# Last feed-forward of a retention and mixture-of-experts kernel: the list scheduler's group time, hand-over times and selection rule

## The chip, the cores and the metric

The kernel runs on one core of a Trainium2 chip. The metric is the device time of one execution in microseconds, as the median of several runs. All times below are microseconds unless marked ns. PE is the matrix engine (TensorE), PEld its weight loads, ACT is ScalarE, DVE is VectorE, POOL is GpSimd and SP is the engine whose queue issues most transfers.

## The reference

The program computes three layers in sequence. The change concerns the third alone, whose width is 512, whose hidden width is 2048, and which has 4608 tokens.

```python
def reference(**kwargs):
    attn_out = _attn_ref(**attn_kwargs)                  # retention, 8 batches x 8 heads x 576 x 64
    x = attn_out.transpose(0, 2, 1, 3).reshape(B * S, H * D)
    x = _moe_ref(x=x, **moe_kwargs)                      # 8 experts, one chosen per token
    return _moe2_ref(x=x, **moe2_kwargs)

def _moe2_ref(x, w_in, w_out):                           # 4608 x 512, 512 x 2048, 2048 x 512
    h = np.maximum(x @ w_in, 0.0)
    return (h * h @ w_out).astype(np.float32)
```

## The kernel before, in words

`phase0` does the retention, `phase12` the experts, `phase3` the last feed-forward. The change lies in `Plan`, the scheduler that `phase3` uses, and in one constant of `phase3`.

**How the work is cut.** `phase3` cuts the tokens into nine tiles of 512 and the hidden width into eight blocks of 256. It goes over the tiles in three passes: pass 0 takes three blocks, pass 1 two and pass 2 three, so that the weights of one pass stay on chip. The second pass goes over the tiles backwards, so the tile at each turn of passes is not loaded again. In pass 0 the tile's input is read, and seven combinations of its four quarters are formed (`xprep`), each split into a high and a low part, by an ACT copy and a DVE subtraction; they are also written to memory (`xc`), from which passes 1 and 2 read them again. Partial outputs go to memory between the passes (`pd`).

**Products.** Each block of a tile is a 2 x 2 block product done with seven products in place of eight, named 1, 2, 6, 5, 7, 4, 3. `one(n, q, x)` makes product x of the first matrix for block q of tile number n, and `two(n, x)` product x of the second matrix. Each is a *group* of six matmuls of 256 columns: two halves, each as high times high, high times low and low times high (lines 1211, 1212 and 1213 of `six`). So a tile has 42 groups in passes 0 and 2, and 28 in pass 1; in all 1008 groups.

**What follows a product.** First products write PSUM banks X (two buffers), Y (two) and Z (one); products 1, 6, 7 and 4 of one block all go through the same X buffer, one after the other. From there ACT copies (L1186) and DVE additions (L1189) form the tile z; it is squared after a relu (`sq`, on DVE as one operation at L1197, or on ACT as two at L1194 and L1195, as the planner chooses), combined (L1189), and split into a high and a low part h (`hsplit`: ACT at L1320, DVE at L1321). z and h have three buffers. Second products read h and write three further banks, X, Y and Z, from which ACT copies or DVE additions bring them into the output tiles `oe` and `yr`. In pass 2 POOL writes finished rows out with indirect transfers (`scatter`).

**The planner.** Nothing of this is issued at once. Each call adds an operation to `Plan.ops`: the engines that can do it with a duration on each, the operations that it must follow (through the names of what it reads and writes), and for transfers a landing time. Durations are formulas: for DVE 0.15 + 0.00106 per column, for ACT 0.21 + 0.00083 per column, for a transfer its size at 320 KB per us plus 2.0 to land, for a group of six matmuls the constant `MMS`. Transfers count as an engine of their own; in the kernel they stand in the queue of SP.

`emit` works in two steps. First it gives each operation a due time. A group of matmuls is due at the sum of the group times in program order ahead of it; another operation is due `SLACK` after that point, and in both cases earlier if what depends on it is due earlier: the due time of the follower, less the operation's duration, landing time and the hand-over to another engine. Then it simulates the engines. An operation among the first 400 that are left is a candidate once all that it must follow has been placed; it can begin when these have ended, with a hand-over added if they ran on another engine, and its engine is free. (`OVER` is the share of an ACT or DVE operation that overlaps the next one.) One candidate is placed at a time, and this selection is part of what the change touches. At the end all operations are issued in the order of their planned starts. On the chip each engine works through its own queue in that order and waits at each operation for what it depends on; the planned times themselves are not used.

Of the kernel before, what the change touches and what calls it, by code (L numbers as in the profile page):

```python
# [92 lines left out]
def kernel(ctx, tc, qT, kT, kN, vN, modT, w_gate, mbias, w1, w2, w_in, w_out,  # L93
# [18 lines left out]
    class Banks:  # L112
        def __init__(self, **tags):
            self.tags = {t: [b, 0] for t, b in tags.items()}
# [974 lines left out]
    AT1 = {1: 0, 2: 1, 6: 3, 5: 5, 7: 6, 4: 9, 3: 11}  # L1089

    class Plan:
        HAND = 0.25
        SLACK = 6.0
        OVER = {"ACT": 0.14, "DVE": 0.11}

        def __init__(self):
            self.ops, self.wrote, self.read = [], {}, {}

        def add(self, engs, fn, r=(), w=(), land=0.0):
            deps = set()  # L1100
            for k in r:
                deps.update(self.wrote.get(k, ()))
            for k in w:
                deps.update(self.wrote.get(k, ()))
                deps.update(self.read.get(k, ()))
            i = len(self.ops)
            self.ops.append((engs, fn, deps, land))
            for k in r:
                self.read.setdefault(k, []).append(i)
            for k in w:  # L1110
                self.wrote[k] = [i]
                self.read[k] = []

        def emit(self, ahead=400, near=0.15):
            n = len(self.ops)
            lat = lambda i: min(t for _, t in self.ops[i][0])
            at, due = 0.0, [0.0] * n
            for i, (engs, _, _, _) in enumerate(self.ops):
                due[i] = at + (0.0 if engs[0][0].name == "PE" else self.SLACK)
                at += engs[0][1] if engs[0][0].name == "PE" else 0.0  # L1120
            for i in range(n - 1, -1, -1):
                engs, _, deps, _ = self.ops[i]
                for d in deps:
                    same = len(engs) == 1 and self.ops[d][0] and self.ops[d][0][0][0] is engs[0][0]
                    due[d] = min(due[d], due[i] - lat(d) - self.ops[d][3] - (0.0 if same else self.HAND))
            free, end, on, starts = {}, {}, {}, []
            todo = list(range(n))
            ready = {}
            while todo:
                cand = []  # L1130
                for i in todo[:ahead]:
                    engs, fn, deps, land = self.ops[i]
                    if i not in ready:
                        if any(d not in end for d in deps):
                            continue
                        ready[i] = [max([end[d] + (0 if on[d] == e.name else self.HAND) for d in deps],
                                        default=0.0) for e, _ in engs]
                    _, s0, e, t = min(((max(r_, free.get(e.name, 0.0)) + t, max(r_, free.get(e.name, 0.0)), e, t)
                                       for (e, t), r_ in zip(engs, ready[i])), key=lambda z: z[:2])
                    cand.append((s0, due[i], i, e, t))  # L1140
                first_ = min(c[0] for c in cand)
                lead = min((c for c in cand if c[0] == first_), key=lambda c: c[1:3])
                s0, _, i, e, t = min((c for c in cand if c[0] <= first_ + near and c[3] is lead[3]),
                                     key=lambda c: c[1:3])
                free[e.name] = s0 + t * (1.0 - self.OVER.get(e.name, 0.0))
                end[i] = s0 + t + self.ops[i][3]
                on[i] = e.name
                starts.append((s0, len(starts), i, e))
                todo.remove(i)
            for s0, _, i, e in sorted(starts, key=lambda z: z[:2]):  # L1150
                self.ops[i][1](e.h)
            self.starts = starts
# [5 lines left out]
    def phase3():  # L1158
        with ExitStack() as c2:
# [3 lines left out]
            for j in (1, 2):  # L1163
# [14 lines left out]
            PE_, ACT_, DVE_, POOL_, DMA_ = (Eng(n_, h_) for n_, h_ in  # L1178
                                            (("PE", pe), ("ACT", act), ("DVE", dve), ("POOL", pool), ("DMA", sp)))
# [28 lines left out]
            def six(ps, pairs, first):  # L1208
                def go(e):
                    for n, ((lh, ll), (rh, rl)) in enumerate(pairs):  # L1210
                        e.matmul(ps[n], lh, rh, start=first and n == 0, stop=False, skip_group_check=True)  # L1211
                        e.matmul(ps[n], lh, rl, start=False, stop=False, skip_group_check=True)  # L1212
                        e.matmul(ps[n], ll, rh, start=False, stop=True, skip_group_check=True)  # L1213
                return go

            MMS = [(PE_, 0.72)]

            def loadw(p, m, j0=0):
                for j, fp in list(enumerate(PASSES[p]))[j0:]:
# [50 lines left out]
            def one(n, q, x):  # L1270
                p, t = T3[n]
                if x == 1:
# [8 lines left out]
                w, m, mx = WT[0][q], MW[x], MX[x]  # L1281
                plan.add(MMS, six([ps, ps], [((w[0][:, m, P * k:P * k + P], w[1][:, m, P * k:P * k + P]),
                                              (XT[mx][:, 0, k, :], XT[mx][:, 1, k, :])) for k in range(2)],
# [48 lines left out]
            def two(n, x):  # L1332
# [4 lines left out]
                for q in range(len(PASSES[p])):  # L1337
                    u = HS_[n, q]
                    h, m, w, mo = HT[u % 3], MH[x], WT[1][q], MO[x]
                    plan.add(MMS, six([ps[:, 0, :], ps[:, 1, :]],  # L1340
                                      [((h[:, 0, m, P * b:P * b + P], h[:, 1, m, P * b:P * b + P]),
# [66 lines left out]
    with tc.manual_schedule():  # L1408
        phase0()
        phase12()  # L1410
        cm.close()
        phase3()
# [37 lines left out]
```

## Time and profile before

| | us |
|---|---|
| median of 3 runs | 1332.95 (1332.58 to 1333.44) |
| the profiled execution | 1330.45 |
| its span, first to last instruction | 1328.7 |
| first matmul of the last feed-forward, from the span's start | 609.7 |
| mean granted TensorE clock | 0.995 |

The span is the time from the first to the last instruction of the profiled execution; the execution's own time is 1.75 longer, and the median of the runs is 2.5 above that. Lines such as L1213 are those of the kernel's listing. A name such as `bank<-x,w` says what an instruction writes and what it reads; in the last feed-forward `x,w` marks first products and `w,h` second products. Matmuls are pipelined, so their durations overlap, and the distance from start to start says how fast they run.

### The profile page before, as it was taken

The numbers are of one execution on the slowest core, as the hardware profiler recorded it, in microseconds if no ns is written. First come the engines' busy times: TensorE is split into PE (matmuls) and PEld (weight loads), VectorE is DVE, ScalarE is ACT, GpSimd is POOL, SyncE is SP. The second block draws the span as 40 slices with busy tenths as digits, with TensorE's granted clock in tenths as the row PEclk, the third lists the DMA queues.
The fourth block names the chain that finished last, engine by engine and source line by source line (L and its number), as shares of the span: only waits on it lengthen the run. The fifth ranks groups of instructions, "written<-read, shape, count | busy, mean of one in ns | idle before, by whom it ended". The sixth has DMA issues, their size and how long they took to land.

```text
span 1328.7 us, 26978 instructions
## 1 busy us (share of the span) xinstructions
PE 1284.4 (97%) x10639; PEld 1196.3 (90%) x10639; DVE 1023.2 (77%) x2095; ACT 623.1 (47%) x1283; POOL 125.3 (9%) x170
## 2 busy tenths in 40 slices
PE   7999989999999999899999999999999999999996
PEld 6888877888888888899999999999999999999996
DVE  3877859878887887665888888867888777777665
ACT  2344444545445444454655556534344344443343
POOL 3222112101100110000000000000000011111121
PEclk9999999999999999899999999999999999999999
DMA  9998257787777877779555554678799866555451
GB/s 330 390 346 300 88 183 245 264 296 272 279 280 264 285 258 270 273 268 351 206 205 221 219 197 175 245 263 309 289 348 345 298 225 211 206 196 175 175 192 47
DMA packets 152499, 331.89 MB, mean 250 GB/s; under 512 B 15440, under 2 KB 67440, under 8 KB 152368
## 3 DMA queue, kind: packets, MB, share of 16 engines
q1 hardware_dynamic: 144752, 309.82, 65.5%
q0 software_dynamic: 5840, 19.14, 4.0%
q8 instruction: 85, 1.39, 0.4%
q10 hardware_dynamic: 1776, 1.17, 0.3%
q14 instruction: 46, 0.38, 0.1%
HBM read 222.33 MB, written 107.78 MB: 248 GB/s over the span
## 4 chain that ended last, share of the span: by engine, by line
PE 40%; DVE 12%; DMA 1%; issue 1%; ACT 0%; POOL 0%; POOLq 0%; DVEq 0%
PE bank L1213 13%; PE bank L1211 13%; PE bank L1212 13%; DVE z L1189 5%; DVE h L1321 3%; DVE z L1197 2%; DMA x<-xc 1%; DVE x L1189 1%; DVE yr L1189 1%; PE bank L839 0%; PE bank L840 0%; PE bank L841 0%; ACT h L1320 0%; DVE oe L1189 0%; POOL out L1328 0%
## 5 line engine op out<-in xcount | busy, mean ns | idle before, releaser
L1211 PE MATMUL bank<-x,w 128*128 128x256 f32 x1008 | 279.6, 277 | 7.5 <-ACT z L1186 5.4
L1212 PE MATMUL bank<-x,w 128*128 128x256 f32 x1008 | 279.4, 277 | 4.4 <-DVE x L1189 4.4
L1211 PE MATMUL bank<-w,h 128*128 128x256 f32 x1008 | 279.9, 278 | 2.6 <-DVE oe L1189 2.0
L1213 PE MATMUL bank<-w,h 128*128 128x256 f32 x1008 | 279.6, 277 | 0.7 <-DVE h L1321 0.7
L1213 PE MATMUL bank<-x,w 128*128 128x256 f32 x1008 | 278.6, 276 | 0.0
L1212 PE MATMUL bank<-w,h 128*128 128x256 f32 x1008 | 278.4, 276 | 0.0
L1186 ACT ACTIVATE z<-bank 128x256 f32<-128x256 f32 x288 | 108.4, 380 | 231.6 <-PE bank L1213 229.9
L1320 ACT ACTIVATE h<-z 128x512 fp32r<-128x512 f32 (+2 forms) x270 | 158.5, 600 | 89.8 <-DVE z L1189 71.1
L1211 PEld LDWEIGHTS bank<-x,w 128*128 128x128 f32 x1008 | 189.3, 188 | 9.4 <-ACT z L1186 6.9
L1212 PEld LDWEIGHTS bank<-x,w 128*128 128x128 f32 x1008 | 189.2, 188 | 6.0 <-DVE x L1189 6.0
L1211 PEld LDWEIGHTS bank<-w,h 128*128 128x128 f32 x1008 | 189.3, 188 | 3.9 <-DVE oe L1189 2.6
L1213 PEld LDWEIGHTS bank<-w,h 128*128 128x128 f32 x1008 | 189.2, 188 | 1.5 <-DVE h L1321 1.4
L1213 PEld LDWEIGHTS bank<-x,w 128*128 128x128 f32 x1008 | 189.3, 188 | 0.1
L1212 PEld LDWEIGHTS bank<-w,h 128*128 128x128 f32 x1008 | 189.3, 188 | 0.0
L1321 DVE TENSOR_TENSOR h<-z,h 128x512 fp32r<-128x512 f32 (+2 forms) x270 | 169.1, 649 | 7.6 <-ACT h L1320 7.6
L1189 DVE TENSOR_TENSOR z<-z,bank 128x256 f32<-128x256 f32 x216 | 89.4, 417 | 64.0 <-PE bank L1213 55.2
L839 PE MATMUL bank<-xh,wx 128*128 128x512 f32 (+3 forms) x320 | 119.5, 373 | 4.1 <-ACT xh L794 2.7
L839 PE MATMUL bank<-hh,wy 128*128 128x512 f32 (+3 forms) x320 | 122.7, 383 | 0.0
L840 PE MATMUL bank<-xl,wx 128*128 128x512 f32 (+3 forms) x320 | 119.2, 373 | 1.0 <-DVE xl L795 1.0
L840 PE MATMUL bank<-hl,wy 128*128 128x512 f32 (+3 forms) x320 | 119.8, 374 | 0.2 <-DVE hl L856 0.2
L841 PE MATMUL bank<-hh,wy 128*128 128x512 f32 (+3 forms) x320 | 119.7, 374 | 0.0
L841 PE MATMUL bank<-xh,wx 128*128 128x512 f32 (+3 forms) x320 | 119.1, 372 | 0.0
(185 smaller groups left out, 2131.0 us busy)
## 6 DMA issues: line engine op xcount, KB each, us to landing
x<-xc SPq DMA_DIRECT2D x112, 512.0 KB
wr<-w SPq DMA_DIRECT2D x80, 512.0 KB
xc<-x SPq DMA_DIRECT2D x63, 512.0 KB
wc<-cwh SPq DMA_DIRECT2D x16, 896.0 KB
wc<-cwl SPq DMA_DIRECT2D x16, 896.0 KB
w<-wc SPq DMA_DIRECT2D x16, 896.0 KB
pd<-oe SPq DMA_DIRECT2D x24, 512.0 KB
xd<-xs SPq DMA_DIRECT2D x9, 1024.0 KB
```

The costliest lines, as they stand in the source:

```text
L839: pe.matmul(ps, lh, rh, start=first, stop=False)
L840: pe.matmul(ps, lh, rl, start=False, stop=False)
L841: pe.matmul(ps, ll, rh, start=False, stop=last)
L1186: plan.add(a_(c), lambda e: e.activation(o, i, f), r, w)
L1189: plan.add(engs or d_(c), lambda e: e.tensor_tensor(out=o, in0=a, in1=b, op=op), r, w)
L1197: e.scalar_tensor_tensor(out=z, in0=z, scalar=0.0, in1=z, op0=ALU.max, op1=ALU.mult)
L1211: e.matmul(ps[n], lh, rh, start=first and n == 0, stop=False, skip_group_check=True)
L1212: e.matmul(ps[n], lh, rl, start=False, stop=False, skip_group_check=True)
L1213: e.matmul(ps[n], ll, rh, start=False, stop=True, skip_group_check=True)
L1320: plan.add(a_(c), lambda e: e.activation(h[:, 0, a:b], z[:, a + 1:b + 1], AF.Copy), rs, ks[0])
L1321: plan.add(d_(c), lambda e: e.tensor_tensor(out=h[:, 1, a:b], in0=z[:, a + 1:b + 1], in1=h[:, 0, a:b].bitcast(F32), op=ALU.subtract), rs + ...
```

## The change

The constants of the planner change: one hand-over time of 0.25 becomes three (0.20 from PE, 0.10 to PE, 0.05 between others, none on the same engine), the slack goes from 6 to 10, and the time of a group from 0.72 to 0.685. The selection changes too. Before, the planner looked for the earliest possible start, took the engine of that candidate (the earliest due one, if several tie), and among the candidates of that engine that can begin within 0.15 of it placed the one with the earliest due time. Now it places the candidate with the earliest start, over all engines; the due time decides between equal starts, and program order after that.

```diff
     class Plan:
-        HAND = 0.25
-        SLACK = 6.0
+        FROM_PE, TO_PE, HAND = 0.20, 0.10, 0.05
+        SLACK = 10.0
         OVER = {"ACT": 0.14, "DVE": 0.11}
...
+        def hand(self, a, b):
+            if a == b:
+                return 0.0
+            return self.TO_PE if b == "PE" else self.FROM_PE if a == "PE" else self.HAND
...
-        def emit(self, ahead=400, near=0.15):
+        def emit(self, ahead=400):
...
-                    due[d] = min(due[d], due[i] - lat(d) - self.ops[d][3] - (0.0 if same else self.HAND))
+                    due[d] = min(due[d], due[i] - lat(d) - self.ops[d][3]
+                                 - (0.0 if same else self.hand(self.ops[d][0][0][0].name, engs[0][0].name)))
...
-                        ready[i] = [max([end[d] + (0 if on[d] == e.name else self.HAND) for d in deps],
-                                        default=0.0) for e, _ in engs]
+                        ready[i] = [max([end[d] + self.hand(on[d], e.name) for d in deps], default=0.0)
+                                    for e, _ in engs]
...
-                first_ = min(c[0] for c in cand)
-                lead = min((c for c in cand if c[0] == first_), key=lambda c: c[1:3])
-                s0, _, i, e, t = min((c for c in cand if c[0] <= first_ + near and c[3] is lead[3]),
-                                     key=lambda c: c[1:3])
+                s0, _, i, e, t = min(cand, key=lambda c: c[:3])
...
-            MMS = [(PE_, 0.72)]
+            MMS = [(PE_, 0.685)]
```

## Rows read from the trace of the kernel before

**Rows 1.** The page: busy time and share of engines; chain that ended last.
```profile
PE 1284.4 (97%) x10639; PEld 1196.3 (90%) x10639; DVE 1023.2 (77%) x2095; ACT 623.1 (47%) x1283; POOL 125.3 (9%) x170
...
PE 40%; DVE 12%; DMA 1%; issue 1%; ACT 0%; POOL 0%; POOLq 0%; DVEq 0%
```

**Rows 2.** Instructions of L1211 and L1213: durations in ns, first and last start.
```profile
L1211 PE MATMUL bank<-x,w x1008: 276/276/391, 609.7 to 1305.0; 128*128 128x256 f32 x168
...
L1213 PE MATMUL bank<-w,h x1008: 276/276/388, 623.1 to 1321.0; 128*128 128x256 f32 x168
```

**Rows 3.** Windows, one tile of each pass: busy time, instructions, clock, DMA.
```profile
core 0: us, PE busy (x) PEld busy (x) DVE busy (x) ACT busy (x) POOL busy (x), PEclk, DMA share, GB/s
694.20:723.40 29.20, 28.85 (x252) 28.66 (x252) 25.70 (x57) 17.82 (x38) 0.00 (x0) 1.00 0.53 199
909.90:929.20 19.30, 19.30 (x170) 19.23 (x170) 16.32 (x36) 8.16 (x19) 0.00 (x0) 1.00 0.82 294
1092.60:1122.20 29.60, 28.95 (x252) 28.75 (x252) 21.58 (x47) 12.70 (x31) 4.35 (x8) 1.00 0.59 200
```

**Rows 4.** Waits of PE, 610 to 1329: in total, times, longest.
```profile
PE bank L1211 <- ACT z L1186: 5.4, 8, 0.7
...
PE bank L1212 <- DVE x L1189: 4.4, 8, 1.2
...
PE bank L1211 <- DMA x<-xc: 2.0, 1, 2.0
PE bank L1211 <- DVE oe L1189: 2.0, 3, 0.8
...
PE bank L1213 <- DVE h L1321: 0.7, 1, 0.7
PE bank L1211 <- ACT h L1320: 0.6, 1, 0.6
```

**Rows 5.** Timeline of pass 0 around 782: start, duration, idle before and releaser.
```profile
781.16 0.68 DVE L1189 TENSOR_TENSOR x<-yr,x 128x512 fp32r<-128x512 f32 x1
...
781.28 0.28 PE L1211 MATMUL bank<-x,w 128*128 128x256 f32 x1
...
781.90 0.39 PE L1212 MATMUL bank<-x,w 128*128 128x256 f32 x1 [0.35 <-DVE x L1189]
...
782.12 0.28 PE L1213 MATMUL bank<-x,w 128*128 128x256 f32 x1
```

**Rows 6.** Timeline of pass 2 from 1208 to 1211.3.
```profile
1208.03 0.28 PE L1213 MATMUL bank<-x,w 128*128 128x256 f32 x1
...
1208.14 0.28 PE L1211 MATMUL bank<-x,w 128*128 128x256 f32 x1
...
1208.22 0.42 DVE L1189 TENSOR_TENSOR z<-z,bank 128x256 f32<-128x256 f32 x1 [2.32 <-PE bank L1213]
...
1208.34 0.39 ACT L1186 ACTIVATE z<-bank 128x256 f32<-128x256 f32 x1 [0.88 <-PE bank L1213]
...
1208.67 0.43 DVE L1197 SCALAR_TENSOR_TENSOR z<-z 128x256 f32<-128x256 f32 x1
...
1209.13 1.22 DVE L1189 TENSOR_TENSOR z<-z 128x256 f32<-128x256 f32 x3
...
1210.05 0.63 ACT L1320 ACTIVATE h<-z 128x512 fp32r<-128x512 f32 x1 [1.32 <-DVE z L1189]
1210.07 0.28 PE L1213 MATMUL bank<-x,w 128*128 128x256 f32 x1
...
1210.59 0.37 ACT L1186 ACTIVATE z<-bank 128x256 f32<-128x256 f32 x1
...
1211.01 0.39 PE L1211 MATMUL bank<-x,w 128*128 128x256 f32 x1 [0.66 <-ACT z L1186]
...
1211.23 0.28 PE L1212 MATMUL bank<-x,w 128*128 128x256 f32 x1
```

**Rows 7.** DVE's instructions by line, 1092.6 to 1299.7: busy, mean ns, idle before.
```profile
L1189 DVE TENSOR_TENSOR oe<-oe,bank 128x512 f32<-128x512 f32 x21 | 14.4, 686 | 12.6 <-PE bank L1213 12.5
```

## The prediction

> **What bounds the kernel now.** I read the page first. TensorE is busy for 97% of the span, and the chain that ended last is 40% PE and only 12% DVE [rows 1]. That mean mixes three stages, and the change touches only the last feed-forward, so I went to its products. Their first matmul starts at 609.7 and their last at 1321.0 [rows 2]: 711.4 us with the last one's 0.1. The rest of the span is what lies before it, which the planner doesn't touch, and what follows the last product: the last additions, the output writes and the closing of the program.
>
> Next I cut that stage into tiles with the view of windows [rows 3]. One token tile takes 29.20 us in the first pass, 19.30 in the second and 29.60 in the third, at a granted clock of 1.00 in each. It has 42, 28 and 42 groups of six matmuls. A first-pass and a third-pass tile hold the same 252 matmuls and yet differ by 0.40, so PE is not at its floor. DVE is busy 25.70 of 29.20 in pass 0 and 21.58 of 29.60 in pass 2: close behind, but not full.
>
> The view of waits names what PE stood for [rows 4]: eight waits for an ACT copy out of a bank (5.4 us), eight for the low half of an input product made by DVE (4.4), one for a DMA (2.0), three for an output addition (2.0), and two for h (0.7 and 0.6). That is 15.1 us of idle array in 22 waits. One wait costs more than its idle: the array runs a matmul's tail of 0.28 - 0.11 = 0.17 into the gap, and the second matmul after a restart follows by 0.22 instead of 0.11. For the copy: the last matmul before it starts at 1210.07, the restart at 1211.01, the next at 1211.23. That is 1.16 us for two steps worth 0.23, so 0.93 lost for 0.66 idle [rows 6]. For the input product: 781.28, 781.90, 782.12, so 0.84 for 0.23, or 0.61 lost for 0.35 idle [rows 5]. I therefore add 0.27 to each wait.
>
> The 8 copies cost 5.4 + 8 x 0.27 = 7.6 us, and are one in each of eight tiles of pass 2. The 8 input waits cost 4.4 + 2.2 = 6.6, one in each of eight tiles of pass 0. The DMA costs 2.3, the output additions (all in the tail, when no other group is left) 2.8, the two for h 1.8: together 21.1. As a check from the other side: a pass-0 tile less its one wait is 29.20 - 0.61 = 28.59, or 0.681 a group; 1008 groups are 686.4, and 711.4 - 686.4 = 25.0. So some 4 us more sit in waits too short to empty the array. **25 us is all that any order could give back; 14.2 of it recurs every tile.**
>
> **The change part by part.** No instruction is added or removed, except that the square of a block may change engine. What changes is the order in which each engine's queue holds the same work.
>
> *Group time 0.72 to 0.685.* The measured group is 0.681. In a tile of 42 the old plan lets PE fall 42 x 0.039 = 1.64 us behind the real one; the new 42 x 0.004 = 0.17. The old plan's tile is 30.24 long, so real PE overtakes it and stands where the plan saw slack. The same wait in every tile, with the same size, is what such an error looks like. At 1210.05 ACT starts an h copy of 0.63; the bank copy that PE needs is ready 0.3 later and goes second, at 1210.59 [rows 6]. A plan at the real pace sees that bank free only at about 1210.96 + 0.10 and sends another ready group first, if there is one.
>
> *Hand-overs.* PE to ACT: the next group starts at 1208.14 and ACT at 1208.34, so 0.20; the new constant is 0.20, the old 0.25. To PE: the copy of 0.37 from 1210.59 ends at 1210.96, PE restarts at 1211.01, and with the slow second step that is 0.05 + 0.11 = 0.16; new 0.10, old 0.25. DVE to ACT: z is ready at 1209.13 + 1.22 = 1210.35 at the latest for the run of three, of which the second ends some 0.3 earlier, and ACT starts at 1210.05, so 0.05 is of the right size. Same engine: a dependent DVE operation starts at 1208.67 after an end of 1208.64; the plan has 0 [rows 6]. So the new plan is short by 0.06 on a hand-over to PE and by 0.03 on each dependent step of one engine; with three such steps in a z chain that is 0.15, an estimate of what a group still waits that the plan sends without reserve.
>
> *The window of 0.15 goes, the earliest start wins.* Ready operations on a free engine still tie, and the due time decides as before. New is only the case in which an engine is free, something unhurried is ready, and something urgent comes within 0.15. Formerly the engine waited up to 0.15; now the urgent one waits for the whole unhurried one. On DVE that is up to 0.69 for an addition to an output [rows 7]. Bounds: nothing where another group covers PE, 0.69 - 0.15 = 0.54 plus 0.27 where none does. For PE itself the edit is good: it no longer stands for a group that isn't ready. I take nothing net, as DVE has 3.5 idle us a tile in pass 0 and 8.0 in pass 2 [rows 3] to recover in.
>
> *Slack 6 to 10.* It makes later only those due times that no matmul sets earlier: input products of the next tile, output additions. PE does reach into the next tile early (the wait at 781.90 is for one of these products), so this edit alone could worsen the pass-0 wait by one operation of 0.68 [rows 5]; but the plan then takes another group, and I put it at nothing between -0.6 and +0.7 a tile.
>
> *DMA order.* Loads keep their place against each other unless two are ready together. Pass 1 moves 294 GB/s at a DMA share of 0.82 [rows 3]. There a 512 KB load put one place later costs 0.5 MB / 294 GB/s = 1.8 us of its lead, on the queue of SP, behind which all later loads stand; the one DMA wait is 2.3 now. Bounds -2.3 to +3.6 (two places); I take 0. The tail's order is forced by one bank through which three products pass in turn: 0, between -1 and +1.
>
> **Sum.** Of the 14.2 that recur, I let each of the 27 tiles keep one such wait: 27 x 0.15 = 4.1. Gain 14.2 - 4.1 = 10.1. The profiled execution took 1330.45, so 1320.4; the median of the runs lies 2.5 above it, so 1322.9, rounded to **1323**.
>
> A rule against this calibration: the Trainium skill, "TensorE: Matmul & The Clock Gate", section "Back-to-back issue gap", gives a warm isolated gap of N/2.4 + 2.5 ns, 109 ns at 256 columns, so 0.655 a group. By it the new plan would still be 42 x 0.030 = 1.26 us slow per tile, and the gain about half. The rows say 0.681, and the same section says that streams with weight loads differ.
>
> **Rivals.** (1) *The plan is still slower than PE, and half of the waits stay.* A group time under 0.685 by as much as 0.03 would do it. Against it is 0.681 from a whole tile. 14.2 / 2 = 7.1 less 2 for the other errors: 5 off, 1328.
>
> (2) *The waits only move.* Four of the seven first products of a block go through one X bank in turn. If no second product is ready around 1210, no order helps: another bank copy is late by as much. For it: all of PE's matmuls shown from 1208.03 to 1211.23 are first products [rows 6]. Against: in pass 0 the copies hold nothing up, with one wait a tile, for another cause [rows 4, 5]. Time 1332 to 1335, taken as 1333.
>
> (3) *Slower: an unhurried DVE or ACT operation gets in ahead of one that PE needs.* Without the 0.15 reserve and with hand-overs of 0.05 the plan runs DVE at 25.70/28.77 = 89% in pass 0. One such blocking costs 0.54 + 0.27 = 0.81. At one in each of the 18 tiles of passes 0 and 2 that is 14.6, which would eat the gain of 10.1 and leave +4.5; with a second in the nine tiles of pass 0, +11.8. It decides once blockings are more than 12 in all (10.1 / 0.81). Taken as +7: 1340. For it: short waits abound at DVE's 90%; against: PE's choice is planned on the same clock, so most are covered by another group.
>
> (4) *Nearly all goes*, the two waits for h and the DMA's among them: 14.2 + 1.8 + half of 2.3 = 17 off, 1316.
>
> **How the numbers follow.** The forecast has a chance of 0.50, rival (1) 0.08, (2) 0.13, (3) 0.21, (4) 0.08. A measurement of this kernel tells about 0.2%, or 2.7 us, from no change. So faster 0.66, same 0.13, slower 0.21. The range reaches to (4) at 1316 and half into (3), 1337; by itself the forecast runs from 1318 to 1327 (one hand-over more or fewer a tile, the DMA's bounds).
>
> **What would show it.** Right: tiles of 28.6 to 28.9 us in passes 0 and 2; the waits of PE for ACT's z and DVE's x gone or under 0.2 each; the tail's three waits as they are; 609.7 unchanged. Group time: no wait that returns with one size in each tile. Window: DVE's waiting work no longer than now. Wrong: a new releaser of PE with eight or more waits over 0.5; a tile over 29.2 in pass 0; x loads that land after 888 us with more than 2.3 lost; or PE's own group slower than 0.69.

## The result and the profile after

The changed kernel took 1320.48 us in the median of 5 runs (1319.15 to 1321.27), beside 1332.58 for the kernel before: a ratio of 0.9902, 95% interval 0.9890 to 0.9913. The prediction was 1323, range 1316 to 1337, so the forecast time held. Its reason did not: the traces and the experiments below give the gain to another part of the change.

The page of the changed kernel first, the rows that answer to [rows 1]; the changed lines have moved all later ones by three, so L1213 is now L1216.

```profile
PE 1279.2 (97%) x10639; PEld 1193.1 (90%) x10639; DVE 1010.4 (77%) x2075; ACT 629.6 (48%) x1323; POOL 125.1 (9%) x170
...
PE 49%; DVE 3%; DMA 2%; ACT 0%; issue 0%; POOL 0%; SPq 0%; POOLq 0%; DVEq 0%
```

DVE has left the chain, from 12% to 3%, and PE has more of it. Next the first and last starts, as in [rows 2]:

```profile
L1214 PE MATMUL bank<-x,w x1008: 276/276/388, 608.5 to 1296.2; 128*128 128x256 f32 x168
...
L1216 PE MATMUL bank<-w,h x1008: 276/276/386, 622.1 to 1311.4; 128*128 128x256 f32 x168
```

The products take 1311.4 - 608.5 = 702.9 from first to last start, 8.4 less than the 711.3 before. Another 1.2 lies ahead of them. The two profiled executions differ by 9.4, the medians by 12.1: the first was 2.1 under its median and the second 0.6 above. One tile of each pass in the view of windows, as in [rows 3]:

```profile
694.20:722.80 28.60, 28.60 (x254) 28.60 (x254) 25.14 (x56) 17.87 (x39) 0.00 (x0) 1.00 0.55 203
901.50:920.60 19.10, 19.10 (x171) 19.10 (x170) 15.95 (x35) 9.93 (x23) 0.00 (x0) 1.00 0.86 309
1109.10:1139.00 29.90, 28.84 (x252) 28.64 (x252) 21.28 (x47) 12.60 (x31) 4.33 (x8) 1.00 0.56 191
```

A tile of pass 0 is now PE from end to end, 28.60 in place of 29.20. One of pass 1 already was, and takes 19.10 in place of 19.30. A tile of pass 2 has become *longer*, 29.90 in place of 29.60. The waits of PE, as in [rows 4]:

```profile
PE bank L1214 <- ACT z L1189: 7.2, 8, 1.1
PE bank L1214 <- DVE oe L1192: 1.8, 3, 0.8
PE bank L1215 <- DMA w<-wc: 0.8, 1, 0.8
PE bank L1214 <- DMA x<-xc: 0.4, 1, 0.4
PE bank L1216 <- DVE h L1324: 0.3, 1, 0.3
PE bank L1215 <- DVE x L1192: 0.2, 1, 0.2
```

The eight waits for x are gone but for one of 0.2. The eight for ACT's z, which I expected to go, have grown from 5.4 to 7.2. The tail's waits are what they were.

The 1.2 ahead of the first product lies where no line was changed. The granted clock of 540 to 560 is 0.91 after and 0.83 before, each a mean of stretches at 1.00 (2.4 GHz) and at 0.50 (1.2 GHz); first the row of the changed kernel, then that of the kernel before:

```profile
540.00:560.00 20.00, 16.25 (x82) 15.22 (x81) 12.53 (x18) 10.17 (x15) 0.00 (x0) 0.91 0.89 308
```
```profile
540.00:560.00 20.00, 16.26 (x73) 15.05 (x72) 11.69 (x16) 9.29 (x15) 0.00 (x0) 0.83 0.89 312
```

In the same 20 us PE ran 82 instructions and 73. The runs below fall on either side (0.91 with the window lifted for all but PE, 0.83 with the rule alone), so it isn't the cause of the gain.

### The profile page after: what moved, and what is told of

It is laid out like the page before. It is cut to its first block, busy times and chain, and to the rows that moved or that the text cites. A ratio compares the mean times of both kernels' runs of the same rounds, so it can differ in the third digit from the quotient of the medians.

```text
span 1319.2 us, 27015 instructions
## 1 busy us (share of the span) xinstructions
PE 1279.2 (97%) x10639; PEld 1193.1 (90%) x10639; DVE 1010.4 (77%) x2075; ACT 629.6 (48%) x1323; POOL 125.1 (9%) x170
## 4 chain that ended last, share of the span: by engine, by line
PE 49%; DVE 3%; DMA 2%; ACT 0%; issue 0%; POOL 0%; SPq 0%; POOLq 0%; DVEq 0%
PE bank L1216 17%; PE bank L1214 16%; PE bank L1215 16%; DVE z L1192 1%; DVE h L1324 1%; DMA w<-wc 1%; DMA yr<-yd 1%; DMA x<-xc 0%; DVE z L1200 0%; DVE oe L1192 0%; ACT z L1189 0%; POOL out L1331 0%; SPq L1205 0%; PE bank L839 0%; PE bank L841 0%
## 5 line engine op out<-in xcount | busy, mean ns | idle before, releaser
L1216 PE MATMUL bank<-w,h 128*128 128x256 f32 x1008 | 278.8, 277 | 0.4 <-DVE h L1324 0.3
L1216 PE MATMUL bank<-x,w 128*128 128x256 f32 x1008 | 278.3, 276 | 0.0
L1216 PEld LDWEIGHTS bank<-w,h 128*128 128x128 f32 x1008 | 189.2, 188 | 1.1 <-DVE h L1324 1.0
L1216 PEld LDWEIGHTS bank<-x,w 128*128 128x128 f32 x1008 | 189.3, 188 | 0.0
L1323 ACT ACTIVATE h<-z 128x512 fp32r<-128x512 f32 (+2 forms) x270 | 152.2, 596 | 42.5 <-DVE z L1192 40.3
```

Source lines behind the costliest of these rows:

```text
L1323: plan.add(a_(c), lambda e: e.activation(h[:, 0, a:b], z[:, a + 1:b + 1], AF.Copy), rs, ks[0])
```

## The experiments

They ran in three sets, each beside the kernel before on one chip; the chips differ. The kernel before took 1324.56 beside the first set, 1334.48 beside the second and 1322.71 beside the third. Each chip served one set, so what belongs to a chip and what to the occasion can't be told apart, and which chip the first runs had is not on record. Ratios are to the kernel before on the same chip; they are those on record, up to 0.1% from the quotients of the medians shown.

| run | what differs | median | ratio (95%) |
|---|---|---|---|
| e1_rule | before, new selection alone | 1312.61 | 0.9906 (0.9889 to 0.9922) |
| e2_times | before, new group and hand-over times alone | 1327.14 | 1.0015 (1.0006 to 1.0025) |
| e3_group | before, group time 0.685 alone | 1325.50 | 1.0006 (0.9997 to 1.0016) |
| e4_slack6 | changed, slack 6 | 1312.95 | 0.9909 (0.9893 to 0.9926) |
| f1_pe_now | before, window lifted for PE | 1330.96 | 0.9977 (0.9966 to 0.9988) |
| f2_rest_now | before, window lifted for all but PE | 1326.85 | 0.9943 (0.9924 to 0.9962) |
| g0_before | before again, one run | 1334.31 | |
| g1_after | changed again | 1321.57 | 0.9914 (0.9893 to 0.9934) |
| h1_window30 | before, window 0.30 | 1336.52 | 1.0111 (1.0094 to 1.0128) |
| h2_dve_now | before, window lifted for DVE | 1315.41 | 0.9942 (0.9926 to 0.9959) |
| h3_plain | changed, plain writes from SP | 1307.86 | 0.9890 (0.9874 to 0.9907) |
| h4_noload | changed, no reload in pass 2 | 1310.30 | 0.9907 (0.9890 to 0.9923) |

**Which part of the change?** The theory on record was the pace of the plan (A): group and hand-over times. The rivals were the selection (B) and the slack (C).

e1_rule, the selection alone:
```diff
-                first_ = min(c[0] for c in cand)
-                lead = min((c for c in cand if c[0] == first_), key=lambda c: c[1:3])
-                s0, _, i, e, t = min((c for c in cand if c[0] <= first_ + near and c[3] is lead[3]),
-                                     key=lambda c: c[1:3])
+                s0, _, i, e, t = min(cand, key=lambda c: c[:3])
```


> The new selection alone, with the old times and slack. If the plan's pace was the cause of the recurring waits (theory A), the waits stay: PE waits in all 27 tiles as before, total within 3 us of the kernel before (1330 to 1336). If the window of 0.15 was the cause, because it sent groups that were not ready (theory B), most of the gain is here: 1320 to 1324.

e2_times, the changed kernel with the old selection and the old slack:
```diff
-                s0, _, i, e, t = min(cand, key=lambda c: c[:3])
+                first_ = min(c[0] for c in cand)
...
-        SLACK = 10.0
+        SLACK = 6.0
```


> The new group and hand-over times with the old selection and the old slack of 6. Theory A (pace): most of the gain, 1319 to 1324, with the waits for the low half of x in pass 0 gone. Theory B (selection): little, 1329 to 1334.

e3_group:
```diff
-            MMS = [(PE_, 0.72)]
+            MMS = [(PE_, 0.685)]
```


> The kernel before with the group time 0.685 alone. Theory A in its narrow form (it is the drift of 1.64 us per tile): at least two thirds of the gain of 12, so 1320 to 1325, and pass 0 without its wait. If the hand-overs matter as much: 1326 to 1331. Theory B: 1330 to 1335.

e4_slack6:
```diff
-        SLACK = 10.0
+        SLACK = 6.0
```


> The changed kernel with the slack back at 6. Theory A and B: within 2 us of the changed kernel (1319 to 1323), as the slack moves only due times that no matmul sets. If the slack is what helps (theory C): back to 1328 or more. My prediction allowed the slack to cost up to 0.7 us a tile in pass 0, by which this kernel could also be faster than the changed one, 1315.

The selection alone gives 0.94%, as much as the whole change (0.98% and 0.86%). The group time alone gives nothing that can be told, group and hand-over times together cost 0.15%, and the slack is worth nothing that the totals can tell. A and C fall, B stands.

What the group time did is seen in a trace. In e3_group the view of waits has, of PE, no line for x any more, and its first two are

```profile
PE bank L1213 <- DVE h L1321: 7.3, 11, 0.8
PE bank L1211 <- DVE oe L1189: 1.5, 2, 0.8
```

and its tile of pass 0, in the view of windows, is

```profile
700.00:730.30 30.30, 29.40 (x254) 28.87 (x254) 25.73 (x57) 17.60 (x37) 0.00 (x0) 1.00 0.52 192
```

So the wait for x went, as theory A said, and one for h of 0.8 came in its place, once a tile: 30.30, longer than the 29.20 of [rows 3]. That is rival (2), a wait that only moves, in a pass for which I had not considered it. Pass 1 did get shorter: the seven tiles that take 135.5 and 136.8 in the two traces of the kernel before take 133.3, which made up for part of it. With the selection alone (e1_rule) PE has eight waits of note in the whole stretch, and none recurs every tile; first its waits (its L1208 is L1211 before), then a tile of each pass:

```profile
PE bank L1208 <- DVE oe L1186: 2.0, 4, 0.8
PE bank L1209 <- DVE x L1186: 1.0, 1, 1.0
PE bank L1209 <- DMA w<-wc: 1.0, 1, 1.0
PE bank L1210 <- DVE h L1318: 0.6, 2, 0.4
```
```profile
700.00:728.60 28.60, 28.60 (x255) 28.60 (x254) 24.92 (x54) 17.97 (x40) 0.00 (x0) 1.00 0.54 203
910.00:929.00 19.00, 19.00 (x170) 19.00 (x169) 16.07 (x35) 8.00 (x18) 0.00 (x0) 1.00 0.82 304
1105.00:1133.60 28.60, 28.60 (x255) 28.60 (x254) 21.68 (x48) 11.38 (x26) 4.39 (x9) 1.00 0.58 203
```

**Whose window?** f1_pe_now and f2_rest_now split the selection. The edit of f1; f2 has `near` and 0.0 exchanged, and h2_dve_now has "DVE" in the place of "PE":
```diff
-                s0, _, i, e, t = min((c for c in cand if c[0] <= first_ + near and c[3] is lead[3]),
+                s0, _, i, e, t = min((c for c in cand if c[0] <= first_ + (0.0 if lead[3].name == "PE" else near)
+                                      and c[3] is lead[3]),
```


> The kernel before, with the window of 0.15 lifted for PE's own choices alone. If the gain comes from PE no longer planning to stand for a group that isn't ready (theory B1), nearly all of the 0.9% is here. If it comes from DVE and ACT no longer standing idle up to 0.15 with work at hand (theory B2), within 0.2% of the kernel before.

> The kernel before, with the window lifted for every engine but PE. Theory B1: within 0.2% of the kernel before. Theory B2: nearly all of the 0.9%. If PE and the rest share it, both this and the run with PE alone show a part, and the parts add to about 0.9%.

> The kernel before with the window lifted for DVE alone. Lifted for DVE, ACT, POOL and transfers together it gave 0.57%, with pass 0 at 232.7 us in place of 236.0. If it is DVE, the fullest of them at 88% in pass 0, the same is here: pass 0 near 232.7. If it is ACT or the transfers, pass 0 stays near 236.

PE's window is worth 0.23%, that of the rest 0.57%, and DVE's alone 0.58%: ACT, POOL and the transfers have no share that can be told. The parts add to 0.8%, of 0.94%. DVE's acts in passes 0 and 1, PE's in pass 1 alone. f1_pe_now, tiles of passes 0 and 1:

```profile
700.00:729.20 29.20, 28.85 (x255) 28.65 (x254) 25.70 (x55) 17.86 (x37) 0.00 (x0) 1.00 0.52 197
910.00:929.04 19.04, 19.04 (x171) 19.04 (x170) 16.20 (x36) 8.05 (x18) 0.00 (x0) 1.00 0.85 301
```

and h2_dve_now:

```profile
700.00:728.60 28.60, 28.60 (x255) 28.60 (x254) 25.29 (x56) 17.34 (x37) 0.00 (x0) 1.00 0.53 202
910.00:929.20 19.20, 19.20 (x171) 19.20 (x170) 16.12 (x36) 7.91 (x18) 0.00 (x0) 1.00 0.79 291
```

Without DVE's window the wait for x leaves pass 0, but for one of 1.0, and the tile falls to 28.60; without PE's alone it stays, at 29.20. Pass 1 falls with either: the seven tiles that take 136.8 in the kernel before on the same chip take 133.3 in f1_pe_now and 134.2 in f2_rest_now.

What changes on DVE shows in the traces, at the same place of a tile of pass 0, first in the kernel before, then in h2_dve_now:

```profile
765.16 0.42 DVE L1189 TENSOR_TENSOR z<-z,bank 128x256 f32<-128x256 f32 x1
765.61 0.42 DVE L1197 SCALAR_TENSOR_TENSOR z<-z 128x256 f32<-128x256 f32 x1
```
```profile
763.19 0.42 DVE L1190 TENSOR_TENSOR z<-z,bank 128x256 f32<-128x256 f32 x1
763.53 0.69 DVE L1190 TENSOR_TENSOR yr<-yr 128x512 f32<-128x512 f32 x1
764.13 0.42 DVE L1198 SCALAR_TENSOR_TENSOR z<-z 128x256 f32<-128x256 f32 x1
```

Before, the square (L1197, in h2_dve_now L1198) stands right behind the addition that it depends on, and starts 0.45 after it, when the addition has ended. In h2_dve_now an independent operation stands between them; it starts 0.34 after the addition, before that has ended. In the last seven tiles of pass 0 the kernel before and f1_pe_now each have 42 operations of 256 columns whose follower starts only after their end, with 0.454 from start to start in place of 0.336; f2_rest_now and h2_dve_now have 10, e1_rule 11.

The unbroken run of 49 DVE operations that holds the awaited low half of x takes 22.3 before and 21.7 in h2_dve_now, and the tile is shorter by the same 0.6. The planner's formulas fit this: a dependent operation can begin 0.05 after DVE is planned to be free (the share of 0.11 of 0.42 that overlaps), which lies inside the window, and an earlier due time then puts it there. DVE's idle time in these tiles is much the same, 25.6 and 24.2. No run changes these pairs alone. Then the doubled window:
```diff
-        def emit(self, ahead=400, near=0.15):
+        def emit(self, ahead=400, near=0.30):
```


> The kernel before with the window doubled to 0.30. If the window costs by what it makes engines wait for, a double one costs more: passes 0 and 1 longer than before (236 and 135 to 137 us), total 0.3 to 1.0% slower. If what counts is only that the order differs (another order, another luck), the sign is open and the total lies within 0.3% either way.

It costs 1.11%. Passes 0 and 1 are longer, as expected if the window costs by what it makes engines wait for: a tile takes 29.60 and 20.20, beside 29.20 and 19.30 in [rows 3], and the count of 42 is 56 here. Of PE's waits these are the longest; that for yr is one that the kernel before does not have, and they alone do not add up to the loss:

```profile
PE bank L1212 <- DVE x L1189: 2.6, 4, 1.0
PE bank L1211 <- DVE oe L1189: 2.5, 5, 0.8
PE bank L1211 <- DMA x<-xc: 1.7, 1, 1.7
PE bank L1211 <- DVE yr L1189: 1.6, 4, 0.4
```

No window, 0.15 and 0.30 thus stand at 0.991, 1 and 1.011: at these three points the cost grows with the window.

**Where does the gain lie, on one chip?** g0_before and g1_after are the two kernels unchanged.

> The kernel before once more, for a trace on the same chip as the others. In pass 2 it had one wait for ACT's z in each tile (0.93 lost each). If that wait lies in the order of the queues, it is here again, as it is the same program. If it lies in the chip of the first runs, pass 2 has none, and where the total of the kernel before then comes from is to be seen in passes 0 and 1.

> The changed kernel once more, beside the kernel before on this chip. If its 1.35 us a tile in pass 2 lies in the order of the queues, they are here again. If in the chip, pass 2 runs without a wait, the total is near that of the changed kernel with the slack back at 6 (0.991 of the kernel before), and the gain is again 0.9 to 1.0%.

I cut both at the same matmuls, counted in the order of their starts (2016 are eight tiles of pass 0, 1176 seven of pass 1, 1764 seven of pass 2; a turn is the last tile of one pass and the first of the next; the last row is the last tile):

| stretch | g0_before | g1_after | difference |
|---|---|---|---|
| up to the first product | 609.5 | 608.4 | -1.1 |
| pass 0 | 235.96 | 229.95 | -6.0 |
| turn to pass 1 | 50.71 | 48.82 | -1.9 |
| pass 1 | 136.75 | 133.87 | -2.9 |
| turn to pass 2 | 50.42 | 48.83 | -1.6 |
| pass 2 | 209.17 | 209.35 | +0.2 |
| last tile | 32.37 | 31.91 | -0.5 |
| after the last matmul's start | 7.6 | 7.9 | +0.3 |

The sum is -13.5, as are the spans (1332.5 and 1319.0). Pass 2 gives nothing on this chip. In the two traces of the first runs the six stretches of products differ by -5.4, -1.3, -1.3, -1.5, +2.0 and -0.8: there pass 2 even cost something. Cut in the same way, pass 2 takes 207.1 to 210.6 in the six traces of the first runs and of the second set, and 199.9 to 203.9 in the eight of the first and third sets, whatever the kernel. In five of the eight, h3_plain and h4_noload among them, it is 199.92.

**What is late in pass 2?** The trace of the changed kernel shows it. ACT, from 1195.7, and PE, from 1197.4:

```profile
1195.78 0.38 ACT L1189 ACTIVATE z<-bank 128x256 f32<-128x256 f32 x1 [0.98 <-PE bank L1216]
1196.19 0.42 ACT L1189 ACTIVATE z<-z 128x256 f32<-128x256 f32 x1
1198.42 0.38 ACT L1189 ACTIVATE z<-bank 128x256 f32<-128x256 f32 x1 [1.81 <-PE bank L1216]
```
```profile
1197.51 0.28 PE L1216 MATMUL bank<-x,w 128*128 128x256 f32 x1
1198.85 0.38 PE L1214 MATMUL bank<-x,w 128*128 128x256 f32 x1 [1.07 <-ACT z L1189]
```

and the same copies in e4_slack6, on the chip of the first set:

```profile
1137.35 0.39 ACT L1189 ACTIVATE z<-bank 128x256 f32<-128x256 f32 x1 [0.97 <-PE bank L1216]
1137.77 0.42 ACT L1189 ACTIVATE z<-z 128x256 f32<-128x256 f32 x1
1138.09 0.36 ACT L1189 ACTIVATE z<-bank 128x256 f32<-128x256 f32 x1
```

There the second copy follows 0.74 after the first and waits for nothing; here it follows after 2.64, and 0.63 after the end of the last matmul that PE had sent (1197.51 + 0.28). PE and ACT wait for each other's signal: the copy for PE's, PE for the copy's. The semaphore updates of PE say the same. Their usual lag behind the modelled end of a group is 0.01; in pass 2 of the first traces and of the second set one or two in each of eight tiles come late, mostly by 1.2 to 2.0, the least by 0.5, and none in the other eight traces. Here the group that ended at 1196.42 was signalled at 1198.39. It happens while POOL issues the last of a tile's four indirect writes (1196.49 to 1197.48) and SP, 0.3 later, a reload of partial outputs. I tried to part these two. h3_plain writes the rows from SP, not permuted; h4_noload leaves out the reload in pass 2, and with it what passes 0 and 1 summed.

h3_plain:
```diff
-                at = bass.IndirectOffsetOnAxis(ap=ixs[n % 2][:, j:j + 1], axis=0)
-                e.memset(gap, 0.0)
-                made = e.indirect_dma_start(out=out[:, :], out_offset=at, in_=oe[:, j, :], in_offset=None)
...
+                r0 = T3[n][1] * TS + j * P
+                sp.dma_start(out[r0:r0 + P, :], oe[:, j, :])
```


> The changed kernel with the four indirect writes of POOL per tile in pass 2 replaced by four plain writes from the queue of SP, to rows that are not permuted; the plan and the orders of PE, ACT and DVE are those of the changed kernel. Theory P: PE's late signals in pass 2 come from POOL's indirect writes; then, on a chip where the kernel before takes some 1333, they are gone, the stretch of pass 2 from 1070 falls from 209 to about 200 us and the total from about 1321 to 1312. Theory L: they come from the reload of partial outputs that SP issues at that moment; then they stay at 1.3 us or more and the total is within 3 us of the changed kernel. On a chip where the kernel before takes some 1324.5 there is nothing to remove: within 2 us of the changed kernel.

h4_noload:
```diff
-                if p and T3[n - 1][1] != t:
+                if p == 1 and T3[n - 1][1] != t:
                     v = VO[n]
```


> The changed kernel without the reload of partial outputs in pass 2, so that what passes 0 and 1 summed is left out of the result; the indirect writes stay. Theory L: PE's late signals in pass 2 are gone, and on a chip where the kernel before takes some 1333 the total falls by about 9 against the changed kernel. Theory P: they stay, once a tile. On a chip where the kernel before takes some 1324.5: within 2 us of the changed kernel.

Both ran on a chip where the kernel before takes 1322.71, so nothing was late there, and neither run can tell the theories apart. What they do show is that queues of PE, ACT and DVE as in the changed kernel give 199.92 in pass 2 on this chip and 209.35 on the other; e4_slack6, which leaves out neither transfer, has 199.92 too.

The traces of the late signals speak against theory L. In all six the eighth comes where no reload is issued. In the kernel before, the group that ended at 1295.68 was signalled at 1296.94, where DVE was waiting; POOL issues the fourth write of a tile, and SP no transfer from 1290 to 1300:

```profile
1295.08 0.97 POOL L1328 DMA_INDIRECT out<-yr,ix  x1 [0.19 <-issue]
1296.97 0.42 DVE L1189 TENSOR_TENSOR z<-z,bank 128x256 f32<-128x256 f32 x1 [2.34 <-PE bank L1213]
```

So the reload isn't needed. That the writes are the cause isn't shown: signals beside a tile's second and third write come on time.

## Why the prediction was right in its time and wrong in its reason

**What bounds the kernel** was read rightly in pass 0: the waits for x were order, and the order cured them, 6.0 of the 6.6 priced. In pass 2 the 7.6 were put down to the plan's pace. They are PE's late signals, one in each of eight tiles: in [rows 6] the addition at 1208.22 starts late, as the group that ended at 1206.95 was signalled at 1208.20, and the h copy and the bank copy follow from it. The waits are there under either order: 7 of 7.0 in all in g0_before, 8 of 7.2 in the changed kernel, of which the six longest cost 1.35 each with the 0.27. On the other chips none of the eight traces has a wait of PE in the seven tiles of pass 2. The kernel before was not traced there, so that its own waits are absent on those chips is inferred from its total, which is 8 to 12 lower, and from e3_group, which has its total and 199.92 in pass 2.

**Group time** is the step that failed. "The same wait in every tile, with the same size, is what such an error looks like" was an argument from a pattern, and any steady plan repeats its waits. With the pace corrected alone, the ratio was 1.0006. The drift of 1.64 was worked out rightly; that removing it removes the waits was not so. In pass 0 the wait moved to h and the tile grew by 1.1, while pass 1 gained 2.2 to 3.5 in all. Nor were the eight waits for x of one size: two are of 1.2 and six of 0.35.

**Hand-overs** were measured at the right size, and the sizes bought nothing: with the group time they gave 1.0015. The 0.15 that the new plan is short of did not come back in every tile; PE has no wait at all from 640 to 838 in g1_after.

**The window** I took at nothing net, between 0 and a loss of 0.81 a time. It is the whole gain: 0.94%, with 0.58 of it on DVE and 0.23 on PE. My bounds had a gain for PE only in words and none for DVE. What I overlooked is that a window also puts dependent operations next to each other on an engine that is 88% busy, at 0.12 each, some six in a tile of pass 0 against one or two without it; the low half of x, late in DVE's unbroken run, came 0.6 later, about what they cost. h1_window30 shows the cost growing with the window. Why PE's window costs pass 1 its 3.5 is not shown.

**Slack** at nothing: right in the total (0.9909 beside 0.9902 and 0.9914). In the traces pass 0 took 232.6 with slack 6 and 229.9 to 230.6 with 10, too little to be told in the time.

**DMA order and tail** at nothing: the tail's three waits stayed, and the waits for loads went from 2.0 to 1.2. The turns gained 2.8 in the first runs and 3.5 on the second chip, more than the 2.3 of my bound; what part of it is loads is not shown.

**The gap of 0.655 a group** from the Trainium skill ("TensorE: Matmul & The Clock Gate", section "Back-to-back issue gap") isn't what runs here, as that section itself says of streams with weight loads: a full tile of 42 groups takes 28.60 in the row above, 0.681.

**The sum**: 10.1 were forecast, as 14.2 less 4.1. On one chip pass 0 gave 6.0, pass 2 nothing, and what I had priced at zero gave 6.9 (turns, pass 1 and last tile), and 1.1 lay outside the stage. The total held because two errors of opposite sign met.

## What to carry to other kernels

A list scheduler whose selection may hold an engine for something not yet ready should be tried first without that liberty; here 0.15 us of it cost 0.9% and 0.30 cost 2%, while times made true to the chip gave nothing by themselves. On an engine that is nearly full, an independent operation between two dependent ones is worth a look. A wait that returns in every tile says that the order is steady, not what is wrong with it: change one constant at a time and see whether it goes or moves. And before a recurring wait is charged to the order, the same program should be traced on another chip. The new selection with the old times (e1_rule) is as fast as the whole change; none of the runs that do all the work beats the two.

## What the runs showed of the hardware that was not expected

The kernel before differs by 0.6 to 0.9% between chips, 1332.58 and 1334.48 on two occasions against 1324.56 and 1322.71 on two. In the traces some 7 to 9 us of it are in pass 2, where completion signals of PE's groups come up to 2.0 us late at one moment of a tile, in all six traces of two occasions and in none of the eight of the other two. PE meanwhile goes on with what it has in its queue. It happens without a reload beside it; whether the indirect writes set it off is open, as leaving them out was tried once, on a chip that doesn't show it.

On DVE, in the rows shown above, an operation that depends on the 128x256 one before it started 0.45 after it, an independent one 0.34. Over seven tiles the means are 0.454 where the follower waits for the end and 0.336 where it doesn't.
